# Retention and two expert layers on one core: banks, pace and order of the weight conversions

## The chip, the cores and the metric

One core of a Trainium2 chip runs the whole program. The time is the device time of one execution in microseconds (us); lower is better. TensorE multiplies, VectorE (DVE), ScalarE (ACT) and GpSimd (POOL) work on the results, and SyncE (SP) issues nearly all DMAs. Each engine, and SyncE's DMA queue too, works through its own instructions in order.

## The reference

```python
scores = scale * q @ k.T                       # 4 batches, 8 heads, 576 positions, 64 per head
ret = scores * Dmat                            # gamma_h ** (i - j) for i >= j, else 0
x = (ret @ v) -> (2304, 512)
h = x @ w_in;  g = h * sigmoid(1.702 * h);  x = g @ w_out        # 512 -> 2048 -> 512
h = x @ w2_in; s = h * softmax(h)                                # 512 -> 1024
out = layernorm(s) * g_ln @ w2_out                               # 1024 -> 512
```

The inputs are float32 in the host's hands; the weights arrive as 64-bit words and are brought to float32 on the chip.

## The kernel before

**Work.** Attention runs first (16 units of two heads, in eight pairs k = 0 to 7). Then the first expert layer runs in 24 steps, `STEPS`: four rounds (`GENS`) of a quarter of the hidden units, in each round three pairs of 384-token blocks, and for each pair two steps i = 0, 1. Step s is 6 x round + 2 x pair + i. A step is `emit_h` (the product with w_in, slice n = 2 x round + i) and `emit_y` (products with w_out). The second layer follows, two token tiles at a time.

**h.** `emit_h` uses Strassen's scheme in Winograd's form for a 2x2 block product: seven groups of six matmuls (each float32 product is three passes of a split into a high and a low part), in the order A, C, B, A, C, D, B. A, C, B and D are four PSUM banks with the tag "s", taken in a ring of four. ScalarE copies A (L736) and C (L740) after their first group; VectorE adds (L728). The add of c12 reads B, and B's second group may start only after it. The gates (`gate`) are two ScalarE passes and one subtraction on GpSimd, or on VectorE in steps 1 and 3 (L702).

**y.** `emit_y` adds up products over four slices (twelve matmuls each) in four banks, by default with the tag "y", a second ring of four. The second token block's y in steps 0, 1 and 3 uses "s" banks. A first result is copied by ScalarE (L801), a later one added by VectorE (L803: in step 1 and in rounds 1 to 3). In rounds 1 to 3 the step i = 0 has y of the second token block of the pair before, and i = 1 that of the first block of its own.

**x.** `combine_x` makes seven combinations of a pair's tokens (four VectorE sums of 128x768, L670 and L298), which ScalarE and GpSimd split (L677, L679) and SyncE stores. In round 0 the sums for the next pair stand between h and y of the steps i = 0, the splits within h of the steps i = 1. Later rounds load the stored parts (`load_x`) within h of the steps i = 1.

**Weights.** A piece of raw words (512 KB, two buffers) is converted by three VectorE passes through a PSUM bank (`convert`, L279, L285, L290); slices of w_in need four subtractions (`queue_combine`, L298), and ScalarE and GpSimd split the result (`split`, L304, L305). The second layer's weights are split in `spill` through the tile `ws` and stored in DRAM; w2_out has a fourth VectorE pass, the scaling with g_ln (L294).

**Order.** All of this stands in a background list (`add`) with costs: 3 for a conversion, 4 with scaling, 0.5 for a subtraction, 0 for splits, loads and spills. `slot(n)` takes from the list until n is used up; a piece that must wait for another holds the list. `slot` stands inside h (n = 0, after the second group of A), behind h and in front of y (`pace(s, 0)`), and behind y (`pace(s, 1)`). Splits and spills that are "late" come out in the next slot, three at most; no spill comes out in a step i = 1 that loads x (`quiet`). A slot issues the stores of its spills before it takes from the list. The list is filled round by round by `queue_gen`.

Of the kernel before, what the change touches and what calls it, by code (L numbers as in the profile page):

```python
# [21 lines left out]
DM = H * D  # L22
# [128 lines left out]
LATE = 3  # L151
PACE = ((2, 6), (6, 0), (5, 0), (6, 3), (6, 3), (6, 3))


class Build:
    def __init__(self, tc, ctx, att, consts, ident_in, w1, w2in, w2out, out):
        self.tc, self.nc = tc, tc.nc
        self.att_in, self.const_in, self.ident_in = att, consts, ident_in
        self.w1_in, self.w2in_in, self.w2out_in, self.out = w1, w2in, w2out, out
        self.ctx = ctx  # L160
        self.mem = self.pool("mem").tile([P, CMEM], F32, name="mem")
        self.wop = self.pool("wo")
# [12 lines left out]
        self.bg, self.late, self.held, self.stores, self.done = [], [], [], [], set()  # L175
        self.gfree, self.gt = list(range(8)), {}
        self.quiet = False
        self.yps = {}
# [87 lines left out]

    def convert(self, raw, dst, scale=None, psum="s"):

        nc = self.nc
        words = raw.rearrange("r (n w) -> r n w", w=2)
        low, high = words[:, :, 0], words[:, :, 1]
        out = self.at(dst, 512)
        at = {}

        def first():
            at["x"] = x = self.ybank("conv") if psum == "y" else self.bank("conv")
            nc.vector.tensor_scalar(  # L279
                x.bitcast(U32), high, 3, 0x3FFFFFF8, ALU.logical_shift_left, ALU.bitwise_and  # L280
            )

        def second():
            x = at["x"].bitcast(U32)
            nc.vector.scalar_tensor_tensor(x, high, 0xC0000000, x, ALU.bitwise_and, ALU.bitwise_or)  # L285

        def third():
            x = at["x"].bitcast(U32)
            to = x if scale is not None else out.bitcast(U32)
            nc.vector.scalar_tensor_tensor(to, low, 29, x, ALU.logical_shift_right, ALU.bitwise_or)  # L290

        p = [first, second, third]
        if scale is not None:
            p.append(lambda: nc.vector.tensor_scalar_mul(out, at["x"], scale))  # L294
        return p

# [13 lines left out]
    def slot(self, n):  # L310
# [15 lines left out]
        ready = lambda need: all(x in self.done for x in need)  # L326
# [6 lines left out]
        while self.bg:  # L333
# [25 lines left out]
    def pace(self, s, part):  # L359


        g, i = divmod(s, 6)
        if g == 0:
            return PACE[i][part]
        slots = [(t, b) for t in range(6) for b in range(2) if b == 0 or t not in (1, 3)]
        if g == GENS - 1:
            slots = [x for x in slots if x < (4, 1)]
        slots = [x for x in slots if x >= (i, part)]
        if (i, part) not in slots:
            return 0  # L370
        n = -(-self.left() // len(slots))
        return n if g == GENS - 1 else min(n, 6)

    def queue_convert(self, raw, dst, scale=None, need=(), give=None, psum="s"):
        p = self.convert(raw, dst, scale, psum)
        self.add(len(p), lambda: [fn() for fn in p], need, give)

# [33 lines left out]

    def next_raw(self, dst, scale=None, need=(), give=None):


        i = self.taken
        self.taken += 1
        self.queue_convert(self.raw(i), dst, scale, tuple(need) + (("raw", i),), give)
        if i + 2 < len(self.pieces):
# [4 lines left out]
    def queue_pair(self, n):  # L423
# [4 lines left out]
        for c in range(2):  # L428
            self.next_raw(_M["stg"] + c * DM, None, before)
        self.queue_combine()  # L430
        self.queue_in(n, gate)
        for c in range(2):
            self.next_raw(OUT_AT + c * DM, None, (("out", 2 * n - 2 + c),))
            self.queue_out(2 * n + c)

    def park(self, i):

        if i < NIN:
            return self.ws[:, i % 2]
# [4 lines left out]

    def spill(self, u, i, src):


        w = self.park(i)
        self.split(w[:, 0], w[:, 1], src)
# [4 lines left out]
    def queue_spill(self, u, src, give=None, need=()):  # L454
        i = self.spills
        self.spills += 1
        self.add(0, lambda: self.spill(u, i, src), need, give, "spill")

    def queue_w2out(self, i):

        g = self.const("g_ln")
        for c in range(2):
            j = 2 * i + c
            k = j % 3
            need = ("r", 1, k) if j < 3 else ("sp", j - 3)
            self.next_raw(W2_AT[k], g[:, j:j + 1], (need,))
            self.queue_spill((i, c), self.at(W2_AT[k], DM), ("sp", j))

    def queue_w2in(self, c):
# [3 lines left out]
        for k in W2IN:  # L473
            self.next_raw(W2_AT[k], None, before(k))
        v = lambda o, a, b, need=(): self.add(1, lambda: self.sub(s(o), s(a), s(b)), need)
# [481 lines left out]
    def prepare(self):  # L957
# [20 lines left out]
        order = [("w1", 1, 2), ("w1", 1, 3)]  # L978
        order += [("w1", n, c) for n in (2, 3) for c in range(4)]
        for g in range(2):  # L980
            order += [("w1", 4 + 2 * g + n, c) for n in range(2) for c in range(4)]
            order += [("in", k, g) for k in W2IN]
        order += [("out", i, c) for i in range(NOUT) for c in range(2)]
# [11 lines left out]
        for c in range(2):  # L995
            self.queue_convert(self.raw(c), _M["stg"] + c * DM, psum="y")
        self.queue_combine()
        self.queue_in(0)
        for c in range(2):
            self.queue_convert(early_out[c], OUT_AT + c * DM, psum="y")  # L1000
            self.queue_out(c)
        self.add(0, lambda: swap("win1"))
        self.queue_convert(late_in[0], _M["stg"], None, (("in", 0),), None, "y")
        self.queue_in(1, (), slice(0, 1))
        self.queue_convert(late_in[1], _M["stg"] + DM, None, (("in", 0),))
# [4 lines left out]
    def queue_gen(self, g):  # L1010

        if g == 0:
            for c in range(2):
                self.next_raw(OUT_AT + c * DM, None, (("out", c),))
                self.queue_out(2 + c)
        if g < GENS - 1:
            self.queue_pair(2 * g + 2)
            self.queue_pair(2 * g + 3)
            if g:
                self.queue_w2in(g - 1)  # L1020
        else:
            for i in range(NOUT):
                self.queue_w2out(i)

    def run(self):
# [40 lines left out]
        for k in range(NPAIR):  # L1066
# [34 lines left out]
            else:  # L1101
# [40 lines left out]
        for g, p, i in STEPS:  # L1142
            s = 6 * g + 2 * PAIRS[g].index(p) + i
            at = PAIRS[g].index(p)
            if s % 6 == 0:
                self.queue_gen(g)
            after = PAIRS[g][at + 1] if at + 1 < NPR else None
# [46 lines left out]
            self.slot(self.pace(s, 1))  # L1194
        for fn in y1[:6] + y2[:4]:
            fn()
# [126 lines left out]
```

## Time and profile before

| | before |
|---|---|
| time, median of 2 runs | 696.55 us (695.88 to 697.22) |
| the profiled execution | 698.53 us |
| its span, first to last instruction | 696.7 us |
| TensorE matmuls busy | 656.1 us, 94% |
| VectorE busy | 454.2 us, 65% |
| ScalarE, GpSimd busy | 278.9 us, 309.1 us |
| mean granted TensorE clock | 0.971 |

Times in the rows are microseconds from the start of the span. Step 0 begins at 65.96, step 4 at 163.3, step 6 at 186.2, step 13 at 295.4, step 19 at 392.9, the second layer at 492.3.

### The profile page before, as it was taken

To read this page: it belongs to the slowest core of one execution; us is meant where nothing else is said; L and a number is where in the kernel's file an instruction comes from. 1 tells how busy PE (TensorE), PEld (TensorE's weight loads), DVE (VectorE), ACT (ScalarE), POOL (GpSimd) and SP (SyncE) were. 2 spreads that over 40 slices of the span, in tenths; PEclk is the share of its full clock that TensorE was granted. 3 is DMA by queue.
4 is the path that set the end of the run, shared out by engine and by line. 5 is a ranking of instruction groups with operands and counts; after the bars stand their busy time and mean duration, and the time that the engine had idled before them with its cause. 6 is when DMAs were issued, how large, how long until landed. Compare 5 with 4: busy or idle time off the path is not lost.

```text
span 696.7 us, 11308 instructions
## 1 busy us (share of the span) xinstructions
PE 656.1 (94%) x4326; PEld 611.9 (88%) x4326; DVE 454.2 (65%) x752; ACT 278.9 (40%) x606; POOL 309.1 (44%) x314
## 2 busy tenths in 40 slices
PE   9997975869999999999999899799999999999997
PEld 8996875859999999998999899799888888888886
DVE  3789876771166664684755645546599877877780
ACT  3564562534543332352333324134354344452331
POOL 3787494762546334582242726246233224331300
PEclk9998998979999999999999989899999999999999
DMA  8997366380047472296740495948800000000001
GB/s 348 417 416 312 122 241 271 106 328 5 0 140 329 144 301 84 91 344 264 290 190 31 193 386 177 363 171 318 328 15 1 32 31 31 26 20 16 31 30 47
DMA packets 30006, 121.78 MB, mean 175 GB/s; under 512 B 3328, under 2 KB 3840, under 8 KB 29952
## 3 DMA queue, kind: packets, MB, share of 16 engines
q1 hardware_dynamic: 29808, 120.99, 45.1%
q8 instruction: 34, 0.56, 0.3%
q14 instruction: 20, 0.16, 0.1%
q10 hardware_dynamic: 144, 0.07, 0.0%
HBM read 88.28 MB, written 32.77 MB: 174 GB/s over the span
## 4 chain that ended last, share of the span: by engine, by line
PE 75%; DVE 12%; DMA 5%; issue 4%; ACT 2%; POOL 2%; SPq 0%; DVEq 0%; ACTq 0%; POOLq 0%
PE y L794 21%; PE o L948 14%; PE h L858 12%; PE h_B L722 6%; PE h_A L722 6%; PE h_C L722 5%; DVE mem L298 3%; PE h_D L722 3%; PE zT L922 2%; DMA x<-xd 2%; DVE conv L285 2%; PE s L591 1%; PE o L606 1%; DVE conv L279 1%; POOL ws L305 1%
## 5 line engine op out<-in xcount | busy, mean ns | idle before, releaser
L702 POOL TENSOR_TENSOR g<-mem,g 128x384 fp32r<-128x384 f32 x86 | 89.7, 1057 | 177.0 <-ACT mem L701 169.1
L728 DVE TENSOR_TENSOR mem<-h_B,mem 128x384 f32<-128x384 f32 x48 | 26.6, 555 | 88.4 <-PE h_B L722 88.4
L794 PE MATMUL y<-g,wo 128*128 128x384 f32 x432 | 78.9, 337 | 0.0
L305 POOL TENSOR_TENSOR win<-mem,win 128x256 fp32r<-128x256 f32 (+2 forms) x59 | 53.3, 929 | 54.9 <-ACT win L304 50.8
L794 PEld LDWEIGHTS y<-g,wo 128*128 128x128 f32 x432 | 76.1, 190 | 0.3 <-DVE mem L803 0.2
L803 DVE TENSOR_TENSOR mem<-y,mem 128x384 f32<-128x384 f32 x76 | 38.7, 552 | 35.3 <-PE y L794 35.0
L794 PE MATMUL y<-g,wo0dt.float32r 128*128 128x384 f32 x216 | 43.1, 344 | 7.2 <-DVE mem L290 7.0
L736 ACT COPY mem<-h_A 128x384 f32<-128x384 f32 x24 | 11.5, 479 | 88.6 <-PE h_A L722 88.6
L679 POOL TENSOR_TENSOR x<-mem,x 128x384 fp32r<-128x384 f32 x42 | 45.4, 1111 | 2.7 <-ACT x L677 2.6
L794 PEld LDWEIGHTS y<-g,wo0dt.float32r 128*128 128x128 f32 x216 | 38.4, 193 | 9.2 <-DVE mem L290 7.5
L298 DVE TENSOR_TENSOR mem<-mem 128x256 f32<-128x256 f32 (+2 forms) x49 | 44.9, 951 | 0.7
L305 POOL TENSOR_TENSOR ws<-mem,ws 128x512 fp32r<-128x512 f32 (+1 forms) x32 | 36.1, 1143 | 16.3 <-ACT ws L304 16.3
L858 PE MATMUL h<-ut,win 128*128 128x512 f32 x168 | 42.9, 391 | 0.0
L948 PE MATMUL o<-u,zs 128*128 128x512 f32 (+1 forms) x171 | 41.7, 388 | 0.0
L794 PE MATMUL y<-g,wo1dt.float32r 128*128 128x384 f32 x216 | 41.7, 342 | 0.0
L909 POOL TENSOR_TENSOR mem<-mem 128x1 f32<-128x1 f32 x18 | 10.3, 572 | 68.8 <-DVE mem L908 62.6
L948 PE MATMUL o<-wo,zs 128*128 128x512 f32 (+1 forms) x171 | 40.0, 378 | 0.0
L864 DVE TENSOR_TENSOR mem<-h,mem 128x512 f32<-128x512 f32 x36 | 24.6, 687 | 22.5 <-PE h L858 12.6
L794 PEld LDWEIGHTS y<-g,wo1dt.float32r 128*128 128x128 f32 x216 | 39.2, 194 | 0.0
L858 PEld LDWEIGHTS h<-ut,win 128*128 128x128 f32 x168 | 31.4, 188 | 6.4
L948 PEld LDWEIGHTS o<-wo,zs 128*128 128x128 f32 x171 | 31.0, 188 | 6.0
L794 PE MATMUL y<-g,wo2dt.float32r 128*128 128x384 f32 x144 | 28.8, 347 | 7.2 <-DVE mem L290 7.2
(155 smaller groups left out, 1531.8 us busy)
## 6 DMA issues: line engine op xcount, KB each, us to landing
x<-xd SPq DMA_DIRECT2D x42, 768.0 KB, 10.3
xd<-x SPq DMA_DIRECT2D x21, 768.0 KB, 7.7
mem<-in_w SPq DMA_DIRECT2D x28, 512.0 KB, 4.7
in<-in_att SPq DMA_DIRECT2D x16, 576.0 KB, 7.9
in<-in_att SPq DMA_DIRECT2D x16, 544.0 KB, 8.0
out<-mem SPq DMA_DIRECT2D x17, 256.0 KB, 2.0
mem<-in_w2in SPq DMA_DIRECT2D x8, 512.0 KB, 7.7
wdt<-ws SPq DMA_DIRECT2D x8, 512.0 KB, 2.7
```

Of the source, the lines that this page charges most:

```text
L285: nc.vector.scalar_tensor_tensor(x, high, 0xC0000000, x, ALU.bitwise_and, ALU.bitwise_or)
L298: self.nc.vector.tensor_tensor(o, a, b, ALU.subtract)
L305: (engine or self.nc.gpsimd).tensor_tensor(lo, src, f32(hi), ALU.subtract)
L679: (engine or self.nc.gpsimd).tensor_tensor(x[:, 1, k], a[:, k], f32(x[:, 0, k]), ALU.subtract)
L702: engine.tensor_tensor(gs[:, 1], u, f32(gs[:, 0]), ALU.subtract)
L722: nc.tensor.matmul(o, w[:, c:c + P], x[j][:, m, k], start=(start and i == 0), stop=(stop and i == 5), skip_group_check=True,)
L728: add = lambda o, a, b: nc.vector.tensor_tensor(o, a, b, ALU.add)
L794: nc.tensor.matmul(o[m], w[:, c:c + P], gs[:, b], start=(begin and i == 0), stop=(end and i == 2),)
L803: nc.vector.tensor_tensor(y[:, m], o[m], y[:, m], ALU.add)
L858: nc.tensor.matmul(o, a[:, l, k], w[:, m], start=(start and i == 0), stop=(stop and i == 5), skip_group_check=True,)
L864: add = lambda o, a, b: nc.vector.tensor_tensor(o, a, b, ALU.add)
L948: nc.tensor.matmul(o[:, 0:n], z[:, a, k], w[:, b, p * n:(p + 1) * n], start=(k == 0 and i == 0), stop=(k == FB - 1 and i == 2),)
```

## The change

- `convert` takes its bank from `self.ring`, or from an explicit function. The ring is "s" except in the slot behind y, where it is "y", and there "s" again in steps 0, 2 and 4. The scaling pass leaves `convert`; ScalarE multiplies in place in `split` (`scale`).
- `PACE` of steps 1 and 3 is (0, 6) in place of (6, 0). The slot of attention pair 6 has 2 in place of 2.4.
- The list is filled once (`queue_rest`), with the weights of the second layer's first product between the rounds' slices one round earlier, and `pace` shares what is left over all slots up to step 22. In the last round nothing caps it.
- Stores of spills are issued at the end of the slot, and a slot takes one spill, in the last round two.
- In steps 0 and 2, two of the four sums of `combine_x` stand behind the slot that follows y.

```diff
-PACE = ((2, 6), (6, 0), (5, 0), (6, 3), (6, 3), (6, 3))
+PACE = ((2, 6), (0, 6), (5, 0), (0, 6), (6, 3), (6, 3))
...
-    def convert(self, raw, dst, scale=None, psum="s"):
+    def convert(self, raw, dst, psum=None):
...
+        x = (psum or self.ring)("conv").bitcast(U32)
+        nc.vector.tensor_scalar(x, high, 3, 0x3FFFFFF8, ALU.logical_shift_left, ALU.bitwise_and)
+        nc.vector.scalar_tensor_tensor(x, high, 0xC0000000, x, ALU.bitwise_and, ALU.bitwise_or)
+        nc.vector.scalar_tensor_tensor(
+            self.at(dst, 512).bitcast(U32), low, 29, x, ALU.logical_shift_right, ALU.bitwise_or
+        )
...
-    def split(self, hi, lo, src, engine=None):
+    def split(self, hi, lo, src, scale=None):
+        if scale is not None:
+            self.nc.scalar.mul(src, src, scale)
         self.nc.scalar.copy(hi, src)
-        (engine or self.nc.gpsimd).tensor_tensor(lo, src, f32(hi), ALU.subtract)
+        self.nc.gpsimd.tensor_tensor(lo, src, f32(hi), ALU.subtract)
...
-            if i >= LATE or (spill and (self.quiet or len(self.stores) > 1)):
+            if i >= LATE or (spill and (self.quiet or len(self.stores) > self.last)):
...
-        for fn in self.stores:
-            fn()
-        self.stores = []
         ready = lambda need: all(x in self.done for x in need)
...
+        for fn in self.stores:
+            fn()
+        self.stores = []
...
-        g, i = divmod(s, 6)
-        if g == 0:
-            return PACE[i][part]
-        slots = [(t, b) for t in range(6) for b in range(2) if b == 0 or t not in (1, 3)]
-        if g == GENS - 1:
-            slots = [x for x in slots if x < (4, 1)]
-        slots = [x for x in slots if x >= (i, part)]
-        if (i, part) not in slots:
+        if s < len(PACE):
+            return PACE[s][part]
+        slots = [(t, b) for t in range(s, NSTEP - 1) for b in range(2) if b == 0 or t % 6 not in (1, 3)]
+        slots = [x for x in slots if x >= (s, part)]
+        if not slots or slots[0] != (s, part):
             return 0
         n = -(-self.left() // len(slots))
-        return n if g == GENS - 1 else min(n, 6)
+        return n if self.last else min(n, 6)
...
+    def queue_rest(self):
+
+        for c in range(2):
+            self.next_raw(OUT_AT + c * DM, (("out", c),))
+            self.queue_out(2 + c)
+        for g in range(1, GENS):
+            self.queue_pair(2 * g)
+            self.queue_pair(2 * g + 1)
+            if g < GENS - 1:
+                self.queue_w2in(g - 1)
+        for i in range(NOUT):
+            self.queue_w2out(i)
...
-                self.slot((0, 0, 0, 0, 3, 3, 2.4, 6)[k])
+                self.slot((0, 0, 0, 0, 3, 3, 2, 6)[k])
...
-                for fn in sums:
+                for fn in sums[:2]:
                     fn()
...
             self.done.add(("y", s))
+            self.ring = self.bank if g == 0 and i == 0 else self.ybank
             self.slot(self.pace(s, 1))
+            self.ring = self.bank
+            if g == 0 and i == 0 and at + 1 < NPR:
+                for fn in sums[2:]:
+                    fn()
```

## Rows read from the trace of the kernel before

**Rows 1.** Busy by stretch: length, PE, PEld, DVE, ACT, POOL, granted clock, DMA.

```profile
78.09:163.30 85.21, 64.26 (x320) 60.48 (x319) 58.82 (x77) 35.67 (x71) 53.19 (x43) 0.88 0.58 219
295.40:321.83 26.43, 23.90 (x133) 22.70 (x133) 17.16 (x27) 12.12 (x25) 18.49 (x15) 1.00 0.98 368
392.90:492.33 99.43, 92.59 (x499) 91.69 (x499) 54.89 (x94) 32.66 (x73) 42.86 (x41) 0.93 0.75 284
```

**Rows 2.** TensorE's waits: waiting line, cause, total, times, longest.

```profile
PE y L794 <- DVE mem L290: 14.2, 5, 6.1
PE h_D L722 <- DVE mem L294: 3.7, 1, 3.7
PE h_B L722 <- DVE mem L290: 3.6, 1, 3.6
PE h_B L722 <- DVE mem L294: 3.1, 1, 3.1
PE s L591 <- DVE mem L290: 2.9, 1, 2.9
PE h_B L722 <- DVE mem L728: 2.4, 1, 2.4
```

**Rows 3.** TensorE's timeline, steps 1 to 3: start, length, line, count, idle before.

```profile
93.93 2.29 PE L722 MATMUL h_B<-x,win1dt.float32r 128*128 128x384 f32 x6 [3.64 <-DVE mem L290]
...
119.93 1.20 PE L722 MATMUL h_C<-x,win0dt.float32r 128*128 128x384 f32 x6
120.97 1.20 PE L722 MATMUL h_B<-x,win0dt.float32r 128*128 128x384 f32 x6
...
139.18 1.32 PE L722 MATMUL h_B<-x,win1dt.float32r 128*128 128x384 f32 x6 [2.44 <-DVE mem L728]
```

**Rows 4.** VectorE's timeline, steps 0 and 1.

```profile
76.23 1.54 DVE L298 TENSOR_TENSOR mem<-mem 128x256 f32<-128x256 f32 x4
...
85.35 6.39 DVE L298 TENSOR_TENSOR mem<-mem 128x768 f32<-128x768 f32 x3
...
104.91 4.75 DVE L298 TENSOR_TENSOR mem<-mem 128x256 f32<-128x256 f32 x4
109.59 0.68 DVE L279 TENSOR_SCALAR conv<-mem 128x512 uint32<-128x512 uint32 x1
...
111.71 0.69 DVE L279 TENSOR_SCALAR conv<-mem 128x512 uint32<-128x512 uint32 x1
```

**Rows 5.** GpSimd's timeline, steps 0 and 3.

```profile
88.94 1.99 POOL L305 TENSOR_TENSOR wo2dt.float32r<-mem,wo2dt.float32r 128x512 fp32r<-128x512 f32 x1
...
132.92 17.29 POOL L679 TENSOR_TENSOR x<-mem,x 128x384 fp32r<-128x384 f32 x14 [1.97 <-ACT x L677]
```

**Rows 6.** DMA issues of the page: what, count, size, median us to landing.

```profile
mem<-in_w SPq DMA_DIRECT2D x28, 512.0 KB, 4.7
```

**Rows 7.** VectorE's timeline, steps 19 to 22.

```profile
397.45 0.75 DVE L294 TENSOR_SCALAR mem<-conv,mem 128x512 f32<-128x512 f32 x1 [1.44 <-POOL ws L305]
...
436.30 0.69 DVE L279 TENSOR_SCALAR conv<-mem 128x512 uint32<-128x512 uint32 x1 [4.70 <-DMA mem<-in_w2out]
...
467.20 2.06 DVE L803 TENSOR_TENSOR mem<-y,mem 128x384 f32<-128x384 f32 x4 [2.43 <-PE y L794]
```

**Rows 8.** Groups by shape, ScalarE: count, busy, mean ns, idle before.

```profile
L540 ACT ACTIVATE in<-in,mem 128x256 f32<-128x256 f32 x32 | 14.3, 500 | 16.1 <-DMA in<-in_att 15.8
```

**Rows 9.** ScalarE's timeline, steps 22 and 23.

```profile
464.81 0.62 ACT L304 CAST ws<-mem 128x512 fp32r<-128x512 f32 x1 [1.55 <-DVE mem L294]
469.46 0.48 ACT L736 COPY mem<-h_A 128x384 f32<-128x384 f32 x1 [4.03 <-PE h_A L722]
```

**Rows 10.** The line of the x loads in step 9: starts and landing.

```profile
L689 SPq DMA_DIRECT2D x<-xd x7: 383/422/1737, 237.3 to 241.6; - x7
...
DMA to landing us min/median/max: 6.2/9.0/13.0
```

**Rows 11.** TensorE's timeline at the end of h in step 10.

```profile
254.82 1.22 PE L722 MATMUL h_B<-x,win 128*128 128x384 f32 x6
```

More of the change, by code (lines that the diff above doesn't have):

```diff
@@ L176, in __init__ @@
         self.gfree, self.gt = list(range(8)), {}
-        self.quiet = False
+        self.quiet = self.last = False
+        self.ring = self.bank
         self.yps = {}
@@ L273, in convert @@
         low, high = words[:, :, 0], words[:, :, 1]
[L274 to L295, printed above, removed]
+        x = (psum or self.ring)("conv").bitcast(U32)
[4 more added lines that the diff above has]
+        )
     def sub(self, o, a, b):
@@ L359, in pace, with queue_convert @@
     def pace(self, s, part):
-        g, i = divmod(s, 6)
-        if g == 0:
-            return PACE[i][part]
-        slots = [(t, b) for t in range(6) for b in range(2) if b == 0 or t not in (1, 3)]
-        if g == GENS - 1:
-            slots = [x for x in slots if x < (4, 1)]
-        slots = [x for x in slots if x >= (i, part)]
-        if (i, part) not in slots:
+        if s < len(PACE):
[3 more added lines that the diff above has]
+        if not slots or slots[0] != (s, part):
             return 0
         n = -(-self.left() // len(slots))
-        return n if g == GENS - 1 else min(n, 6)
-    def queue_convert(self, raw, dst, scale=None, need=(), give=None, psum="s"):
-        p = self.convert(raw, dst, scale, psum)
-        self.add(len(p), lambda: [fn() for fn in p], need, give)
+        return n if self.last else min(n, 6)
+    def queue_convert(self, raw, dst, need=(), give=None, psum=None):
+        self.add(3, lambda: self.convert(raw, dst, psum), need, give)
     def queue_combine(self):
@@ L428, in queue_pair @@
         for c in range(2):
-            self.next_raw(_M["stg"] + c * DM, None, before)
+            self.next_raw(_M["stg"] + c * DM, before)
         self.queue_combine()
@@ L432, in queue_pair, with park @@
         for c in range(2):
-            self.next_raw(OUT_AT + c * DM, None, (("out", 2 * n - 2 + c),))
+            self.next_raw(OUT_AT + c * DM, (("out", 2 * n - 2 + c),))
             self.queue_out(2 * n + c)
-    def park(self, i):
-        if i < NIN:
+    def park(self):
+        i = self.spills = self.spills + 1
+        if not self.last:
             return self.ws[:, i % 2]
@@ L443, in park, with spill @@
         return self.win[2][:, i * SLICE:(i + 1) * SLICE].rearrange("r (a b) -> r a b", a=2)
-    def spill(self, u, i, src):
-        w = self.park(i)
-        self.split(w[:, 0], w[:, 1], src)
+    def spill(self, u, src, scale):
+        w = self.park()
+        self.split(w[:, 0], w[:, 1], src, scale)
         self.stores.append(
@@ L452, in spill, with queue_spill @@
         )
[L454 to L457, printed above, removed]
+    def queue_spill(self, u, src, give=None, need=(), scale=None):
+        self.add(0, lambda: self.spill(u, src, scale), need, give, "spill")
     def queue_w2out(self, i):
@@ L473, in queue_w2in @@
         for k in W2IN:
-            self.next_raw(W2_AT[k], None, before(k))
+            self.next_raw(W2_AT[k], before(k))
         v = lambda o, a, b, need=(): self.add(1, lambda: self.sub(s(o), s(a), s(b)), need)
@@ L978, in prepare @@
         order = [("w1", 1, 2), ("w1", 1, 3)]
[L979 to L982, printed above, removed]
+        for g in range(1, GENS):
+            order += [("w1", 2 * g + n, c) for n in range(2) for c in range(4)]
+            if g < GENS - 1:
+                order += [("in", k, g - 1) for k in W2IN]
         order += [("out", i, c) for i in range(NOUT) for c in range(2)]
@@ L995, in prepare @@
         for c in range(2):
-            self.queue_convert(self.raw(c), _M["stg"] + c * DM, psum="y")
+            self.queue_convert(self.raw(c), _M["stg"] + c * DM, psum=self.ybank)
         self.queue_combine()
@@ L1008, in prepare @@
         self.queue_in(1, (), slice(1, 3))
[L1010 to L1019, printed above, removed]
+    def queue_rest(self):
+        for c in range(2):
+            self.next_raw(OUT_AT + c * DM, (("out", c),))
+            self.queue_out(2 + c)
+        for g in range(1, GENS):
+            self.queue_pair(2 * g)
+            self.queue_pair(2 * g + 1)
+            if g < GENS - 1:
                 self.queue_w2in(g - 1)
-        else:
-            for i in range(NOUT):
-                self.queue_w2out(i)
+        for i in range(NOUT):
+            self.queue_w2out(i)
     def run(self):
@@ L1144, in run @@
             at = PAIRS[g].index(p)
-            if s % 6 == 0:
-                self.queue_gen(g)
+            if s == 0:
+                self.queue_rest()
+            self.last = g == GENS - 1
             after = PAIRS[g][at + 1] if at + 1 < NPR else None
@@ L1193, in run @@
             self.done.add(("y", s))
+            self.ring = self.bank if g == 0 and i == 0 else self.ybank
             self.slot(self.pace(s, 1))
+            self.ring = self.bank
+            if g == 0 and i == 0 and at + 1 < NPR:
+                for fn in sums[2:]:
+                    fn()
         for fn in y1[:6] + y2[:4]:
```

14 lines of the change are left out of this document (7 added, 7 removed).

## The prediction

> **What bounds the kernel now.** Start with the table of busy times by stretch and compare each stretch with the work in it [rows 1]. TensorE's own pace is in its timeline: a group of six matmuls starts 1.04 us after the one before [rows 3], so the seven h groups of a step take 7.28 us, and a slice of y (twelve matmuls at that pace) 2.08. From y of step 0 to the end of step 3 stand sixteen slices and three h: 33.3 + 21.8 = 55.1 us. The stretch takes 85.2 at a mean granted clock of 0.88: **30.1 us lost**. From h of step 13 to h of step 14 (two h, four slices, 22.9 us) 3.5 are lost of 26.4. From h of step 19 to the start of the second layer (five h, 24 slices, 86.3) 13.1 are lost of 99.4. The rest of the first layer holds no long wait, and the second layer is not touched.
>
> The waits of TensorE say who ended the lost time [rows 2]: VectorE, five times in front of y by the third pass of a conversion (14.2 us), once each in front of h_B and h_D by a conversion (3.6) or by its scaling (3.1, 3.7), once by an add of h (2.4), once in attention's scores by a conversion (2.9). The rest of the loss is clock: after a wait of 3.64 us six matmuls took 2.29 us, nearly twice the usual 1.20, after one of 2.44 us they took 1.32 [rows 3]. In VectorE's timeline look at what stood in its queue then [rows 4]: before y's second half in step 1 four subtractions (4.75 us) and two conversions (one starts 2.12 after the other), before h_B of step 1 three sums (6.39).
>
> **The change, part by part.**
>
> *Attention, 2.4 becomes 2.* The four subtractions use up the 2, so one conversion leaves the slot that scores waited for 2.9 us [rows 2], and all later ones come one place later. VectorE's chain of scan, masks and h gets a conversion shorter: 2.1 us. Bounds: 0 (another wait takes its place) and 4 (the 2.9 and slow matmuls behind). I take **2**.
>
> *Steps 0 to 3.* Following the list with the new paces, five conversions and one set of four subtractions that ran before the end of step 3 run in steps 4 to 6, where VectorE had none: 5 x 2.1 + 1.5 to 4.75 = 12 to 15 us of queue less. What is left, step by step:
> - Behind y of step 0 come two conversions and only then two sums. h_B of step 1 needs the first conversion's bank, free at y's end plus 2.1, as h_B starts: the 3.6 go. But the add that h_B's second group waits for is behind 4.2 of conversions and two sums at 6.39/3 = 2.13: late by 1.8.
> - GpSimd's queue: the splits of w_out slices 2 and 3 (1.99 each [rows 5]) now stand behind three parts of x instead of before them, so the first y slice of step 1 waits 1.7.
> - Nothing stands in front of the second half of y in step 1 or 3: its 14.2, nearly all of it, goes, with the slow matmuls behind. The work moves after y. There the two conversions follow the 2.06 of y's adds [rows 7], done 5.3 after y's end; h's seventh group could start 6.24 after it, so nothing is lost while the load has landed (median 4.7 us [rows 6], issued a slot ahead). That is the cover; without it each late us is paid.
> - Step 2 keeps four subtractions (I take 2.4), a conversion (2.1), and four sums (1.4 + 3 x 2.13); the next h's add is queued behind them. With h's own three adds this is 14 us after h ends; the seventh group of step 3 could start after 4.16 + 6.24 = 10.4. Late by 3.5, and by the 3.64 us row a slow spell of about 2.
>
> Left: 1.8 + 1.7 + 3.5 + 2 + 0.4 for bank copies = 9.4; gained **20.7**. Ends: 28 if no add is late; 10 if the subtractions take 4.75 again, every sum is at its dearest, and each stall has its slow spell.
>
> *One list, even pace.* The 103 units that are left at step 6 go over 28 slots, four each at first; weights for the second layer's first product go two to three steps earlier. No slice is wanted before it comes: slice 4's split is queued in step 9 for step 12, 5's in step 11 for 13, 6's in 15 for 18, 7's in 17 for 19. Spills of the first product: one per slot, its store behind the slot's loads, in place of two in each of three slots of step 12, which held ScalarE and SyncE's queue and so the x loads of step 13. The 3.5 us of steps 13 and 14 go: **3.5** (ends 0 and 3.5).
>
> *Banks behind y.* In steps 18 and 20 the conversions after y took h's banks; h_B (3.1) and h_D (3.7, its conversion first idle 4.70 on a load [rows 7]) waited. Now they take y's, which VectorE has just emptied, and h never waits for a bank behind y. One conversion per slot also gives each load one more slot. Gain: the 13.1, say **12.9**.
>
> *ScalarE scales w_out.* Eight passes of 0.75 us [rows 7] leave VectorE; ScalarE gets eight of about 0.62, as a 128x512 cast of it takes [rows 9], between 0.50 for half the width [rows 8] and twice that. Seven run with time around them. The eighth, slice 7's, is emitted before h of step 23, behind a conversion that ends 2.1 after y's adds; ScalarE then has pass and cast in front of the copy of h_A that started at 469.46 [rows 9]: about 473.0 instead of 471.3 for the fourth h group. Cost **1.7**, ends 0.5 and 3. The Trainium skill (ScalarE: Activation LUTs, Rules for kernel authors) says to multiply on VectorE, not on ScalarE. The page's formula (What ACT_TABLE_LOAD costs) makes such a pass 0.71 us, an estimate, and the cost 1.8; no row here shows this pass.
>
> *SyncE's queue.* x for the next pair is loaded in steps 7, 9, 13, 15, 19, 21, behind the loads and now the store of the slot before. In step 9 this left no slack: seven x loads went out at 237.3 to 241.6, the first 6.2 and the last 13.0 us under way [rows 10], so the last landed at 254.6, and the group that reads it started at 254.82 [rows 11]. Parts of 768 KB thus land 1.85 apart, and a store of 512 KB in front costs 1.3. I count half of it, 0.7, in five steps, since the store can go while the first x buffers are still being read: cost **3.5**, ends 0 and 7.
>
> **Sum.** 2 + 20.7 + 3.5 + 12.9 - 1.7 - 3.5 = 33.9. The profiled execution took 698.53 (span 696.7 and 1.8 around it): 664.6. The median of the runs shown is 2.0 below it: **662.5**.
>
> **Rivals.**
> - *VectorE's queue is the bound of steps 0 to 3 and the waits only move.* VectorE was busy 58.8 of those 85.2 us [rows 1], and GpSimd's x splits (14 in 17.29 [rows 5]) run beside the sums. For it: four subtractions took 1.54 us with GpSimd idle and 4.75 beside the splits [rows 4]; the sums put back behind conversions fall into the splits. Against: five conversions less. Then steps 0 to 3 give 10, the rest 10 to 13: 674 to 678. SBUF — State Buffer, Who interferes with whom, in the Trainium skill states the mechanism: a VectorE operation with both inputs in SBUF and a GpSimd one that reads SBUF shut each other out for a whole instruction. The two rows on four subtractions agree.
> - *The change doesn't reach the bound*: a wait in front of y with another name, POOL's gates or ScalarE's, keeps 25 of the 30 us. For it: five splits now run late. Against: no wait of TensorE on GpSimd is among the longest [rows 2]. Steps 0 to 3 give 5, the rest 10 less 5 for the late splits: about 686.
> - *Slower*: the seven x loads. If SyncE, held by a load that waits for its conversion, starts them late by more than step 9's slack, each us is paid in six steps: 6.2 x 6 eats the 37.4 us of the gains, and from 8.6 on it is slower by 2%, 711 us. For it: a single late train is all it takes in each step. Against: conversions behind y, which hold that queue, end 5.3 after it, within h.
>
> **How the numbers follow.** The forecast 0.68, own range 650 to 672; the first rival 0.22; the second 0.07; the slower one 0.03. Gains at their high ends sum to 48 less 0.5, so 649; taking in the first rival, 679 on the other side: **649 to 679**. About 2% (14 us) is what a measurement can tell: faster 0.90, within 0.07, slower 0.03.
>
> **What would show it.** Right: TensorE's waits of y and h_B on conversions gone, h_D's and h_B's on the scaling gone, step 3 ended 20 us or more earlier; a wait of h_B on an add in steps 1 and 3; a wait of 1 to 2 us on ScalarE's copy of h_A in step 23. Wrong: conversions idle on loads with h_B behind them, waits on x loads above 1 us, a granted clock still below 0.9 before step 4.

## The result, and the profile after

The changed kernel takes **674.05 us** (median of 2 runs, 673.23 to 674.86) against 696.55: a ratio of 0.968 (95% interval 0.961 to 0.974), faster by 22.5 us. The forecast was 662.5 with a range of 649 to 679: the direction and most of the places were right, the gain came out at two thirds of the forecast. The time lies above the 650 to 672 that the forecast gave to its own mechanism, and inside the wide range only because that took in the first rival. The profiled execution took 674.86 us, 23.7 below that of before.

The page of the changed kernel first: its span and TensorE's matmuls and loads, busy time with its share.

```profile
span 673.1 us, 11311 instructions
PE 646.8 (96%) x4326; PEld 602.6 (90%) x4326; DVE 443.6 (66%) x744; ACT 284.0 (42%) x614; POOL 304.6 (45%) x314
```

Busy by stretch, in the columns of [rows 1]: y of step 0 to the end of step 3, and h of step 19 to the second layer.

```profile
74.77:141.66 66.89, 59.53 (x319) 57.98 (x319) 50.31 (x69) 35.43 (x70) 50.66 (x42) 0.95 0.53 203
379.70:469.70 90.00, 87.33 (x500) 86.14 (x499) 48.15 (x83) 34.92 (x75) 36.16 (x36) 1.00 0.70 273
```

The first holds 55.1 us of work in 66.9: 11.8 lost where it was 30.1, at a granted clock of 0.95 in place of 0.88. The second fell from 99.4 to 90.0. TensorE's waits, against [rows 2]:

```profile
PE h_B L704 <- DVE mem L710: 6.4, 4, 4.0
PE h_B L704 <- DMA x<-xd: 2.6, 5, 0.6
PE h_B L704 <- DVE mem L278: 2.6, 1, 2.6
PE y L776 <- POOL wo2dt.float32r L292: 2.0, 1, 2.0
PE h_A L704 <- ACT mem L718: 1.7, 1, 1.7
PE h_D L704 <- DMA x<-xd: 1.5, 3, 0.6
```

The 14.2 us of y behind a conversion (L290 before, L278 now) are gone, and the scaling stands in no wait. Adds of h (L710), x loads and single waits on GpSimd and ScalarE stand in their place. In the timeline:

```profile
91.38 1.34 PE L704 MATMUL h_B<-x,win1dt.float32r 128*128 128x384 f32 x6 [0.96 <-DVE mem L710]
94.93 3.32 PE L776 MATMUL y<-g,wo2dt.float32r 128*128 128x384 f32 x11 [2.04 <-POOL wo2dt.float32r L292]
126.58 2.29 PE L704 MATMUL h_B<-x,win1dt.float32r 128*128 128x384 f32 x6 [3.98 <-DVE mem L710]
157.90 1.32 PE L704 MATMUL h_B<-x,win1dt.float32r 128*128 128x384 f32 x6 [2.55 <-DVE mem L278]
448.54 1.32 PE L704 MATMUL h_A<-x,win1dt.float32r 128*128 128x384 f32 x6 [1.72 <-ACT mem L718]
```

These are steps 1, 1, 3, 5 and 23. Four of the five were forecast; the one of step 5 (157.90) was not.

From the starts of h in TensorE's timeline comes the length of every step, the best measure for what follows. In steps 6 to 22, where a step without a wait lasts 15.6 us, a second profile of the same kernel (the control below) differs by 0.5 us at most; in steps 0 to 5 by up to 1.6, so differences under 2 us there are not read. Us:

| step | before | after | control | stores first | one behind | three edits | all, pace 0 | all, one spill |
|---|---|---|---|---|---|---|---|---|
| 1 | 31.0 | 21.1 | 19.6 | 21.1 | 21.1 | 21.1 | 18.2 | 18.2 |
| 3 | 33.0 | 25.5 | 26.7 | 25.5 | 25.6 | 25.4 | 19.8 | 19.8 |
| 4, 5 | 22.9 | 25.7 | 27.3 | 25.7 | 27.0 | 24.9 | 24.2 | 24.2 |
| 9, 10 | 31.2 | 33.9 | 34.1 | 32.4 | 33.8 | 33.1 | 31.2 | 31.2 |
| 11, 12 | 31.2 | 31.2 | 31.2 | 35.5 | 31.2 | 31.2 | 34.3 | 31.4 |
| 13, 14 | 34.7 | 34.6 | 34.5 | 34.4 | 31.2 | 34.8 | 31.2 | 31.2 |
| 15, 16 | 31.6 | 34.5 | 34.0 | 33.2 | 31.2 | 32.2 | 31.2 | 31.2 |
| 17, 18 | 31.2 | 31.2 | 31.2 | 33.6 | 31.2 | 31.2 | 32.9 | 32.9 |
| 19, 21 | 44.1 | 31.2 | 31.2 | 31.2 | 32.5 | 31.2 | 32.5 | 32.5 |
| 23 | 24.1 | 26.1 | 26.1 | 26.1 | 26.1 | 24.1 | 24.1 | 24.1 |
| lost in 6 to 22 | 16.8 | 11.0 | 10.4 | 14.8 | 6.1 | 8.7 | 9.7 | 6.4 |

### The profile page after: what moved, and what is told of

It reads as the page before. It is cut to its first block, busy times and chain, and to the rows that moved or that the text cites. A ratio compares the mean times of both kernels' runs of the same rounds, so it can differ in the third digit from the quotient of the medians.

```text
span 673.1 us, 11311 instructions
## 1 busy us (share of the span) xinstructions
PE 646.8 (96%) x4326; PEld 602.6 (90%) x4326; DVE 443.6 (66%) x744; ACT 284.0 (42%) x614; POOL 304.6 (45%) x314
## 4 chain that ended last, share of the span: by engine, by line
PE 73%; DMA 11%; DVE 10%; issue 2%; POOL 1%; ACT 1%; SPq 1%; POOLq 0%; DVEq 0%; ACTq 0%
PE y L776 20%; PE o L930 15%; PE h L840 13%; DMA x<-xd 10%; PE h_B L704 6%; PE h_A L704 5%; PE h_C L704 5%; DVE mem L283 3%; PE zT L904 2%; PE h_D L704 2%; PE s L573 2%; PE o L588 1%; DVE mem L578 1%; DVE conv L277 1%; DVE conv L276 1%
## 5 line engine op out<-in xcount | busy, mean ns | idle before, releaser
L684 POOL TENSOR_TENSOR g<-mem,g 128x384 fp32r<-128x384 f32 x86 | 88.0, 1033 | 168.5 <-ACT mem L683 158.4
L710 DVE TENSOR_TENSOR mem<-h_B,mem 128x384 f32<-128x384 f32 x48 | 26.6, 555 | 65.8 <-PE h_B L704 61.7
L283 DVE TENSOR_TENSOR mem<-mem 128x256 f32<-128x256 f32 (+2 forms) x49 | 41.8, 881 | 7.0 <-POOL ws L292 6.4
L776 PE MATMUL y<-g,wo0dt.float32r 128*128 128x384 f32 x216 | 40.3, 334 | 0.0
L776 PEld LDWEIGHTS y<-g,wo1dt.float32r 128*128 128x128 f32 x216 | 37.7, 188 | 0.0
L840 PEld LDWEIGHTS h<-ut,win 128*128 128x128 f32 x168 | 31.4, 188 | 6.4
L930 PEld LDWEIGHTS o<-u,zs 128*128 128x128 f32 x171 | 29.9, 189 | 5.2
```

The costliest lines, as they stand in the source:

```text
L283: self.nc.vector.tensor_tensor(o, a, b, ALU.subtract)
L684: engine.tensor_tensor(gs[:, 1], u, f32(gs[:, 0]), ALU.subtract)
L710: add = lambda o, a, b: nc.vector.tensor_tensor(o, a, b, ALU.add)
L776: nc.tensor.matmul(o[m], w[:, c:c + P], gs[:, b], start=(begin and i == 0), stop=(end and i == 2),)
L840: nc.tensor.matmul(o, a[:, l, k], w[:, m], start=(start and i == 0), stop=(stop and i == 5), skip_group_check=True,)
L930: nc.tensor.matmul(o[:, 0:n], z[:, a, k], w[:, b, p * n:(p + 1) * n], start=(k == 0 and i == 0), stop=(k == FB - 1 and i == 2),)
```

## Experiments

Each kernel ran in three rounds beside the kernel before (695.28, 694.54, 694.54 and 696.54 us in the four groups).

**The ring in the slot behind y (e1_ring_s).** The changed kernel with h's banks there.

```diff
-            self.ring = self.bank if g == 0 and i == 0 else self.ybank
+            self.ring = self.bank
```

> The changed kernel with conversions always in h's banks (tag s), behind y too. If the banks behind y earned the 12.9 us of the last round, as the forecast has it, h_B or h_D wait on conversions again in steps 19 and 21 and the time goes to 682 us or more. Rival, the even pace earned it: a single conversion behind y takes the bank of D, which h wants 5.2 us after y's end, and is done by 3.2, so steps 19 to 22 stay at 15.6 to 16.4 us; only steps 2, 4 and 13, behind two conversions, lose 1 to 2 us each: 676 to 679.

Measured: 682.52 us, 0.981 of before (0.977 to 0.985). Steps 19 and 21 stay at 15.6. So the 12.9 us of the last round, which the forecast gave to y's banks, do not hang on them. The likely reason is that with one conversion per slot and its load one slot earlier a bank of either ring is free in time; no run undoes that pace alone. The banks' worth lies elsewhere: steps 2, 6, 10, 13 and 22 lose 0.7 to 1.3 us each (14 gains 1.3), and h_B waits for a conversion three times instead of once.

**The same ring in the kernel before (e2_before_ring).**

```diff
-            at["x"] = x = self.ybank("conv") if psum == "y" else self.bank("conv")
+            at["x"] = x = self.ybank("conv") if psum == "y" else self.ring("conv")
...
+            self.ring = self.bank if g == 0 and i == 0 else self.ybank
             self.slot(self.pace(s, 1))
+            self.ring = self.bank
```

> The kernel before with one thing added: conversions behind y take y's banks (not in steps 0, 2, 4). By the forecast's reading the waits of h_B (3.1) and h_D (3.7) in steps 19 and 21 and the slow matmuls behind them go: 12 to 13 us, 684. Rival, VectorE's queue and the late load hold h, not the bank: the add that the seventh group of h waits for still stands behind the same conversions (it ran at 400.97 and 439.23), so the wait moves to h_B on an add: step 19 gains 3.5 to 6, step 21 about 1, in all 4 to 7: 689 to 692.

Measured: 695.95 us, 1.001 (0.999 to 1.004): nothing. In the profile step 19 goes from 21.8 to 20.8 and step 21 from 22.3 to 18.2, and steps 10, 20 and 22 pay 2.4 of it back; the 3.2 us that steps 6 to 22 keep there do not show in the time. TensorE in step 19:

```profile
401.54 1.31 PE L723 MATMUL h_A<-x,win1dt.float32r 128*128 128x384 f32 x6 [3.30 <-ACT mem L737]
```

and VectorE in steps 19 and 21:

```profile
401.98 0.75 DVE L295 TENSOR_SCALAR mem<-conv,mem 128x512 f32<-128x512 f32 x1 [3.91 <-POOL ws L306]
...
437.29 0.69 DVE L280 TENSOR_SCALAR conv<-mem 128x512 uint32<-128x512 uint32 x1 [3.69 <-DMA mem<-in_w2out]
```

The conversions still wait for a spill and a load; h now waits for something else behind them. The wait moved; freeing the bank alone was worth nothing in the time.

**Conversions in front of y again (e3_front).** The changed kernel with the pace of before in steps 1 and 3.

```diff
-PACE = ((2, 6), (0, 6), (5, 0), (0, 6), (6, 3), (6, 3))
+PACE = ((2, 6), (6, 0), (5, 0), (6, 0), (6, 3), (6, 3))
```

> The changed kernel with the paces of steps 1 and 3 as before, (6, 0): two conversions in front of y there. If their place in front of y was the cost, y waits on a conversion again in both steps, 2 to 4 us each with slow matmuls behind: 679 to 684. Rival, the list did it (the four subtractions no longer stand in these slots): y's second half waits under 1 us and the time is 673 to 676.

Measured: 680.89 us, 0.980 (0.977 to 0.983). Of the 14.2 us of y's waits only this is back:

```profile
PE y L776 <- DVE mem L278: 2.5, 2, 1.5
```

Both waits are in step 3. The reason is in VectorE's timeline of that kernel: the four subtractions of a slice of w_in that stood in front of y in step 1 of before for 4.75 us [rows 4] come out only behind h of step 2 (115.13); those of step 0 stay in step 0 (78.07).

```profile
78.07 3.18 DVE L283 TENSOR_TENSOR mem<-mem 128x256 f32<-128x256 f32 x4
...
98.50 0.68 DVE L276 TENSOR_SCALAR conv<-mem 128x512 uint32<-128x512 uint32 x1
...
115.13 3.19 DVE L283 TENSOR_TENSOR mem<-mem 128x256 f32<-128x256 f32 x4
```

In step 1 the conversions start at 98.50, right after the gates, without the subtractions ahead. With the subtractions elsewhere in the list, the two front slots together cost about 3 us (steps 0 to 3: 81.0 us here, 77.8 and 78.2 in two profiles of the changed kernel). Whether the new pace alone, with the list as before, would have won the 14.2 was not tried.

**The scaling on VectorE (e4_scale_vector).**

```diff
-            self.nc.scalar.mul(src, src, scale)
+            self.nc.vector.tensor_scalar_mul(src, src, scale)
```

> The changed kernel with the scaling of w_out on VectorE, in the same place (in the split of the spill). The engine doesn't matter: 673 to 675, the wait of h_A on ScalarE's copy in step 23 stays at 1.5 to 1.9 us, since the cast behind the scaling still stands in front of the copy. Rival, the scaling pass on VectorE was what the last round lost: 3 us or more slower, with h_B waiting on adds in steps 19 to 23.

Measured: 680.24 us, 0.979 (0.976 to 0.982). Step 23 lasts 26.3 (26.1 after), so the wait there is not the price of ScalarE's pass but of what is flushed ahead of h. Step 20 loses 1.1; most of the rest lies in steps 0 to 5, which the edit does not touch. Nothing speaks for VectorE; the size is left open. The passes:

```profile
L290 ACT ACTIVATE mem<-mem 128x512 f32<-128x512 f32 x8 | 5.8, 723 | 8.8 <-DVE mem L278 8.8
```

```profile
L290 DVE TENSOR_SCALAR mem<-mem 128x512 f32<-128x512 f32 x8 | 3.7, 480 | 0.0
```

The first is ScalarE's in the changed kernel (0.72 us), the second VectorE's here (0.48). The Trainium skill (ScalarE: Activation LUTs, Rules for kernel authors) sends a multiplication to VectorE as the faster engine for it. The two rows agree on the price of one pass; the time of the kernel does not follow it.

**Control (c_after).** The changed kernel, not edited, in the group of the next three edits.

> The changed kernel itself, beside the three others of this group. All theories: 673 to 675 us, about 0.968 of the kernel before; step 1 lasts 21 us, step 5 14.3, step 23 26. It says which of the differences of single steps between runs are worth anything.

Measured: 676.33 us, 0.973 (0.970 to 0.976). Its steps are the measure of noise used above.

**Three edits against the losses of rounds 0 to 3 (b1_three).** Two spills per slot in steps i = 0; one conversion of step 4 moved from in front of y to behind it; the last flush behind h of step 23.

```diff
-PACE = ((2, 6), (0, 6), (5, 0), (0, 6), (6, 3), (6, 3))
+PACE = ((2, 6), (0, 6), (5, 0), (0, 6), (3, 3), (6, 3))
...
-            if i >= LATE or (spill and (self.quiet or len(self.stores) > self.last)):
+            if i >= LATE or (spill and (self.quiet or len(self.stores) > (self.last or n == 0))):
...
-            if s + 1 == NSTEP:
-                self.flush()
...
             if s + 1 == NSTEP:
+                self.flush()
                 self.open_second()
```

> Three edits of the changed kernel: two spills may come out in a step i = 0 (so that a spill no longer shares its slot with the subtraction that overwrites its source), step 4 has one conversion in front of y and one behind it with its own bank ahead of step 5's h (pace 3 and 3), and the stores and splits of the last slot are flushed behind h of step 23. If the losses after round 0 are these: step 5 falls from 14.3 to 11.4, steps 9, 10, 15 and 16 together lose 1 to 2 us instead of 6, step 23 falls from 26 to 24: 8 to 10 us, 664 to 667. Rival, the line of x loads alone sets these steps: step 5 and 23 fall, the others stay, 669 to 671.

Measured: 669.01 us, 0.964 (0.960 to 0.967), 7.3 under the control. Step 23 is whole again (24.1), and so are steps 9 and 15. One spill per slot had put a spill into the slot of the subtraction that overwrites its source; VectorE stood still in step 8 of the changed kernel:

```profile
207.61 0.69 DVE L283 TENSOR_TENSOR mem<-mem 128x512 f32<-128x512 f32 x1
211.50 1.76 DVE L283 TENSOR_TENSOR mem<-mem 128x512 f32<-128x512 f32 x1 [3.21 <-POOL ws L292]
```

and doesn't with two:

```profile
206.57 2.92 DVE L283 TENSOR_TENSOR mem<-mem 128x512 f32<-128x512 f32 x2
```

The loss of step 9 itself is a wait of h_B on an add, which stands in VectorE's queue behind the delayed conversion and two more subtractions:

```profile
221.37 1.34 PE L704 MATMUL h_B<-x,win0dt.float32r 128*128 128x384 f32 x6 [0.77 <-DVE mem L710]
```

Steps 10 and 14 are not helped, and step 22 loses 1.3 more. Step 5 keeps 2.0: h's bank is free, and the gates of GpSimd, behind splits of w_in, hold y for 1.7.

**Stores ahead of the list (e6_stores_first).** As the kernel before issued them.

```diff
+        for fn in self.stores:
+            fn()
+        self.stores = []
         ready = lambda need: all(x in self.done for x in need)
...
-        for fn in self.stores:
-            fn()
-        self.stores = []
```

> The changed kernel, but a slot issues the stores of its spills before it takes from the list, as the kernel before did. If the store behind the slot's loads is what makes x late (the term of 3.5 us): steps 10, 14, 16, 20 and 22 give back 2 to 3.5 us, 670 to 672. Rival, x is late because the loads ahead of it wait for late conversions: no change, within 1 us of the changed kernel.

Measured: 678.68 us, 0.977 (0.974 to 0.980), 2.3 over the control. Steps 10 and 16 give back 1.5 and 1.3, as the first theory said; step 14 does not move (its x loads have no store ahead of them), and steps 11 and 17 lose 4.3 and 2.4. VectorE at the start of step 11:

```profile
250.80 0.69 DVE L276 TENSOR_SCALAR conv<-mem 128x512 uint32<-128x512 uint32 x1 [3.02 <-DMA mem<-in_w]
```

and SyncE's queue ahead of that:

```profile
244.34 0.32 SPq L435 DMA_DIRECT2D wdb<-ws  x1
244.76 1.15 SPq L262 DMA_DIRECT2D mem<-in_w  x2
```

The store waits for its split, which GpSimd ends at 244.3, and the raw load behind it goes out at 244.76, though its buffer was empty at 242.3. The conversion that wants it is 3 us late, and the add of h behind that conversion too. So the order of stores is a trade, and the place of the stores in the change is the better one.

**All four sums in front of y (e9_sums_front).**

```diff
-                for fn in sums[:2]:
+                for fn in sums:
...
-            if g == 0 and i == 0 and at + 1 < NPR:
-                for fn in sums[2:]:
-                    fn()
```

> The changed kernel, but all four sums of the next pair stand in front of y in steps 0 and 2. If the two sums behind the conversions are worth what the steps suggest: the wait of h_B in step 1 on a bank comes back (3 to 4 us, step 1 at 24 to 25 us), step 3 changes by less than 1: 676 to 678. Rival, the order of sums and conversions only exchanges one wait (on a bank) for another (on an add): within 1 us.

Measured: 678.19 us, 0.975 (0.972 to 0.978), 1.9 over the control, with intervals that overlap. The wait on the bank is back in step 1,

```profile
89.45 1.31 PE L704 MATMUL h_B<-x,win1dt.float32r 128*128 128x384 f32 x6 [2.80 <-DVE mem L278]
```

but the step is no longer (20.4): the wait on the add (0.96) and the one on GpSimd's split (2.04) are gone. That is nearer to the rival: one wait is exchanged for others.

**One conversion behind y ahead of x loads (e12_one_behind).**

```diff
-        return n if self.last else min(n, 6)
+        most = 3 if part and s % 6 in (0, 2) else 6
+        return n if self.last and most > 3 else min(n, most)
```

> The changed kernel, but in rounds 1 to 3 the slot behind y of the steps i = 0 that x loads follow takes one conversion and no more. If the x loads of steps 9 and 13 are late because two raw loads, each held until a conversion behind y ends, stand in front of them in SyncE's queue: step 14 falls from 19.0 to 15.6 or 16, step 10 from 17.3 to 16, 4 to 5 us in all, 670 to 672. Rival, the seven x loads take their 13 us at the DMA engines whatever stands in front: steps 10 and 14 change by less than 1, 675.

Measured: 672.77 us, 0.969 (0.965 to 0.972). Steps 9 and 13 to 16 are whole; step 14 goes from 19.0 to 15.6, as the first theory said. Step 10 does not follow (18.2), and steps 19 and 22 lose 1.3 more each. Step 9 is whole although VectorE still waits 3.21 us for a spill in step 8: the two subtractions no longer stand in the slot behind y, ahead of the add. SyncE's queue in step 13 of the changed kernel, DMA issues with their time and count:

```profile
282.44 2.46 SPq L262 DMA_DIRECT2D mem<-in_w  x2
284.99 5.03 SPq L671 DMA_DIRECT2D x<-xd  x7
```

and here:

```profile
283.46 0.33 SPq L262 DMA_DIRECT2D mem<-in_w  x1
283.84 4.29 SPq L672 DMA_DIRECT2D x<-xd  x7
...
291.58 0.33 SPq L262 DMA_DIRECT2D mem<-in_w  x1
```

Each raw load waits for the conversion that empties its buffer. The second conversion behind y ended at 284.54, the second load went out at 284.57, and seven x loads stood behind it. h of step 13 begins at 279.3 there and 280.3 here, so x goes out 5.7 us into the step in place of 3.5, with one load less ahead of it at the DMA engines. The Trainium skill (DMA: Bandwidth & Descriptors, Anatomy of one DMA) says that a DMA's semaphore wait happens on the issuing sequencer, ahead of dispatch; these rows agree: x's own buffers were not what held it.

**All edits (b2_all).** The three, the one conversion, pace 2 in step 2, and:

```diff
-        low = lambda t: nc.vector if s in (1, 3) or s == t == 0 else nc.gpsimd
+        low = lambda t: nc.vector if s in (1, 3, 5) or s == t == 0 else nc.gpsimd
...
                     if g == 0:
+                        if j == 0:
+                            self.slot(0)
                         split(j)
```

> The three edits of b1_three and four more: one conversion behind y in front of x loads, as in e12_one_behind; pace 2 in place of 5 in step 2 (its conversion goes to later steps, the four subtractions stay); in step 1 the splits of w_out are queued ahead of the splits of x; the gates' subtractions of step 5 on VectorE. By the theory: step 1 falls by 2 (the wait of y on GpSimd's split goes), step 3 by 2 to 4 (the add that h_B waits for comes a conversion of 2.1 earlier, and a shorter wait costs less clock), step 5 by 1.7, steps 10, 14, 16 and 22 by 6 together: 12 us under b1_three, 656 to 659. Rival, the queues of VectorE and GpSimd only hand the waits on: 663 to 667.

Measured: 664.28 us, 0.955 (0.952 to 0.958). Steps 1, 3 and 5 give about what was expected (2.9, 2.3 and 2.0 against the three edits; step 1 gives 1.4 against the control, whose step 1 was shorter). In steps 6 to 22 the rival was right: 10, 14 and 16 are whole, but 6, 11, 12, 18 and 19 now wait, and 9.1 us are lost in place of 8.7.

**The same with pace 0 in step 2 (b3_all).**

> As b2_all, but pace 0 in step 2: the four subtractions go as well. By the theory the wait of 4 us in step 3 is gone whole, 2 us under b2_all, if the subtractions behind y of step 3 do not hold step 4's first add or the splits of the third slice of w_in; rival, they do, and step 4 or 5 pays the 2 to 3 us back.

Measured: 661.94 us, 0.953 (0.950 to 0.956). Step 3 falls by 3.3 to 19.8, step 4 pays 1.3 back. The wait of 3.98 us in step 3 was VectorE's queue, in the changed kernel:

```profile
113.77 3.18 DVE L283 TENSOR_TENSOR mem<-mem 128x256 f32<-128x256 f32 x4
...
119.00 1.75 DVE L652 TENSOR_TENSOR mem<-mem 128x768 f32<-128x768 f32 x1
120.78 5.28 DVE L283 TENSOR_TENSOR mem<-mem 128x768 f32<-128x768 f32 x3
125.98 0.55 DVE L710 TENSOR_TENSOR mem<-h_B,mem 128x384 f32<-128x384 f32 x1
```

and without subtractions and conversion it is:

```profile
111.19 0.95 DVE L653 TENSOR_TENSOR mem<-mem 128x768 f32<-128x768 f32 x1
112.25 4.14 DVE L283 TENSOR_TENSOR mem<-mem 128x768 f32<-128x768 f32 x3
117.01 0.56 DVE L711 TENSOR_TENSOR mem<-h_B,mem 128x384 f32<-128x384 f32 x1 [0.62 <-PE h_B L705]
```

The second is the last kernel (below), whose step 3 is the same. The add now waits for TensorE, not TensorE for it.

**The same with one spill per slot (b4_one_spill).**

```diff
-            if i >= LATE or (spill and (self.quiet or len(self.stores) > (self.last or n == 0))):
+            if i >= LATE or (spill and (self.quiet or len(self.stores) > self.last)):
```

> As b3_all, but without the edit of the spills: one spill per slot, as in the changed kernel. In b2_all and b3_all steps 6 to 22 lose about as much as in b1_three, though steps 10, 14 and 16 are whole again, since steps 6, 12 and 18 wait for splits of w_in; the kernel with one conversion in front of x loads alone (e12_one_behind) lost 6 us there with one spill per slot. If the two edits get in each other's way through the order of the list: steps 6 to 22 lose 6 instead of 10, 658 us. Rival, the late splits of w_in come from the pace in steps 2 to 5 and the cap alone, and the spills add nothing: 661 to 663, steps 12 and 18 as in b3_all.

Measured: **658.63 us**, 0.947 (0.944 to 0.950), the fastest of all. Steps 6 to 22 lose 6.4 us, steps 11 and 12 are whole but for 0.2, and step 17 takes step 18's place. Its longest waits on other engines in the first layer:

```profile
PE h_C L705 <- ACT mem L723: 1.5, 1, 1.5
PE h_B L705 <- DVE mem L711: 1.4, 1, 1.4
PE h_B L705 <- DVE mem L278: 1.1, 1, 1.1
```

The first of them is step 1's, where the splits of w_out now stand ahead of ScalarE's copy: part of the 2.04 came back there. The two edits did get in each other's way. The collision of spill and subtraction is not gone: it stands once, in step 16,

```profile
328.04 1.76 DVE L283 TENSOR_TENSOR mem<-mem 128x512 f32<-128x512 f32 x1 [3.21 <-POOL ws L292]
```

and step 17 loses 1.7, with h_B waiting on an add behind four subtractions (the second of the waits above). That is less than the 4.7 us that steps 11, 12 and 18 lose with two spills per slot. How the second spill brings those about was not followed.

## Why the prediction was right, and where it was not

The profiled executions, term by term in us of gain (a step's length before less its length after):

| part | forecast | measured |
|---|---|---|
| attention, and h of step 0 behind it | 2 | 3.3 |
| y of step 0 to the end of step 3 | 20.7 | 18.3 |
| steps 4 and 5 | 0 | -2.8 |
| steps 13 and 14 | 3.5 | 0.1 |
| steps 19 and 21 | 12.9 | 12.9 |
| steps 10, 16, 20, 22 (x loads; the forecast counts 14 in) | -3.5 | -5.0 |
| steps 9, 15 (an add) | 0 | -2.1 |
| step 23 | -1.7 | -2.0 |
| second layer | 0 | 1.0 |
| sum | 33.9 | 23.7 |

**Steps 0 to 3 came close, and their waits were right.** An add late by 1.8 in step 1 (0.96), y behind GpSimd's split by 1.7 (2.04), an add late by 3.5 in step 3 (3.98): 7.0 us in sum, as forecast. The 2.4 us that are missing are mostly clock. The forecast counted a slow spell behind the wait of step 3 (it came: six matmuls in 2.29 us) and none behind those of step 1, where eleven matmuls of y took 3.32 us; in the control, behind the same wait, 2.20. All three waits went when their queue was emptied: the wait on the split by queueing it earlier (step 1 from 21.1, in the control 19.6, to 18.2), the add of step 3 with the queue ahead of it. But the 14.2 us of y's waits were put down to the place of the conversions. With conversions back in front of y, 2.5 of them came back, so the list, which now has the subtractions elsewhere, decides more. That the smaller pace in attention shifted it is argued from the list's order; no run changes that pace alone.

**The last round came out to the tenth, for another reason.** The forecast named y's banks as the cause and one conversion per slot as an aside. Taking the banks away left both steps at 15.6; giving them to the kernel before moved the waits and won nothing in the time; with the scaling on VectorE they last 15.7 and 15.6, with the stores first 15.6 each. What is left is the even pace with its one list, and these two were not taken apart. As far as the banks go, the right number is luck.

**The step that failed is the term of SyncE's queue, with that of steps 13 and 14.** It counted the store, 0.7 us in five steps, and took the 3.5 us of steps 13 and 14 as gone with the spills. The store is a part of it: with the stores first, steps 10 and 16 gave back 1.5 and 1.3 of the 1.7 and 2.3 us that they lose against 15.6. But no store stands ahead of the x loads that step 14 waits for. It lost 3.4 us to a raw load held by a second conversion behind y, and with one conversion there it was whole. The prediction's rival "slower" had that mechanism and set it aside since conversions behind y end 5.3 us after it, within h. They end within h, but h is when x must go out: from 4.3 us into a step nothing was lost before (237.3 in step 9, begun at 233.0 [rows 10]), at 5.7 step 14 lost 3.4. The start alone does not set the loss: in step 9 of the changed kernel x went out 6.0 us into the step, and step 10 lost 1.7. How that 1.7 divides stays open: with the stores first 0.2 of it is left, with the three edits alone or the one conversion alone it is no smaller (1.9 and 2.6), and with all edits it is gone.

**Steps 9 and 15 were not in the forecast.** There h_B waits on an add (0.77 and 0.73 us), behind a conversion that a spill has delayed and two subtractions in the same slot. It takes both: step 9 is whole without the spill's wait, and also with that wait and without the subtractions in the slot.

**Not seen at all: step 5.** The new list brings four subtractions between two conversions of step 4 that take h's banks, and the last pass ends 4.8 us into step 5, where h_B wanted its bank at 2.1:

```profile
152.92 2.81 DVE L283 TENSOR_TENSOR mem<-mem 128x256 f32<-128x256 f32 x4
155.65 0.68 DVE L276 TENSOR_SCALAR conv<-mem 128x512 uint32<-128x512 uint32 x1
156.36 0.70 DVE L277 SCALAR_TENSOR_TENSOR conv<-mem,conv 128x512 uint32<-128x512 uint32 x1
157.16 0.69 DVE L278 SCALAR_TENSOR_TENSOR mem<-mem,conv 128x512 uint32<-128x512 uint32 x1
```

The forecast counted the 12 to 15 us of queue that leave steps 0 to 3 and placed them in steps 4 to 6 "where VectorE had none", at no cost.

**Step 23** cost 2.0 for 1.7, but not by the scaling pass on ScalarE: with the pass on VectorE the step lasted 26.3. It is the flush ahead of h, and goes with its place. The second layer's 1.0 was not looked into.

**The rivals.** The first (waits only move, 674 to 678) gave nearly the time that came, by a mechanism that did not: it had steps 0 to 3 give 10, they gave 18, and the waits that took the gain stood in the steps behind them. The second did not come: one wait of y on GpSimd, 2.0 us, is all that is left of its kind. The mechanism of the third came in one step of its six, at 3.4 us.

## What to carry to other kernels

Work taken off the critical place is not gone: follow the list to the slot where each piece comes out, and cost that slot like the first one. In a queue in order, ask of every DMA what it waits for and what stands behind it; a load that waits for a conversion holds all the loads that wait for nothing. And where several edits meet one wait, undo them one at a time before naming the cause: here the bank was named, and the steps stayed whole without it.

## What the runs showed that was not expected

- What a wait costs TensorE afterwards is not set by its length alone. Six matmuls took 2.29 us after 3.64 [rows 3] and after 3.98, but 1.32 after 2.44 [rows 3] and, in step 5, after 2.55. The wait of step 5 stands at the same length in the control and in the kernel with h's banks behind y, and there the six took 1.79 (the first line) and 2.29 (the second):

```profile
158.97 1.79 PE L704 MATMUL h_B<-x,win1dt.float32r 128*128 128x384 f32 x6 [2.56 <-DVE mem L278]
```

```profile
161.95 2.29 PE L704 MATMUL h_B<-x,win1dt.float32r 128*128 128x384 f32 x6 [2.56 <-DVE mem L278]
```

- The wait of y in step 1 is 2.04 us in both profiles of the changed kernel. Behind it eleven matmuls took 3.32 us in the first and 2.20 in the control, at a mean granted clock of 0.83 and 1.00 (92 to 102 us). Most of the 1.2 to 1.6 us by which steps 1, 3 and 5 differ between the two comes from this: a price of the clock that is read from one row is one of several. In the control:

```profile
96.32 2.20 PE L776 MATMUL y<-g,wo2dt.float32r 128*128 128x384 f32 x11 [2.04 <-POOL wo2dt.float32r L292]
```

- Four subtractions took 3.18 and 2.81 us in the changed kernel, between the 1.54 and 4.75 of [rows 4]. The Trainium skill (SBUF — State Buffer, Who interferes with whom) has the mechanism, an exclusive lock on shared ports; the spread agrees with it.
- In step 13 of the changed kernel seven x loads of 768 KB landed 1.86 us apart on the mean behind the raw load (that at 291.3, the last of the seven at 304.4): 13 us of a step of 15.6. This leaves little room to make up 2 us of delay at their start.
